# One matmul instead of two for the phases of an S4D kernel: the two constants that round a phase move into the same 32 rows as its parts

## The chip, the cores and the metric

The kernel runs on one core of one Trainium2 chip. The metric is the device time of one execution in microseconds (us), the median of a few runs; lower is better.

## The reference

The layer normalises its input and adds three things: the input itself, an S4D convolution and a gated linear unit. L is 2048 positions, D is 448 channels, N is 256 complex modes for each channel, and F is 1792 hidden features.

```python
xn = layernorm(A_u)                                   # [1, 2048, 448]
# S4D
dt = exp(log_dt);  A = -exp(log_A_real) + 1j * A_imag;  C = (C_real + 1j * C_imag) * dt[:, None]
P = exp((A * dt[:, None])[:, :, None] * arange(2048))
K = 2 * einsum("dn,dnl->dl", C, P).real               # one filter per channel
y = irfft(rfft(xn.T, 4096) * rfft(K, 4096))[:2048].T + xn * D_skip
# GLU
h = sigmoid(xn @ w_gate) * (xn @ w_up)                # [2048, 1792]
out = A_u + y + h @ w_down
```

## The kernel before

Two generators are interleaved by a table of weights. One, `conv`, does the S4D part; the other, `glu`, does the gated unit. A scheduler then fixes the order of the instructions of every engine when the program is built, from its own model of durations. Each engine runs its instructions strictly in that order.

**The GLU.** Every weight and activation is split into a high and a low fp32r part, so that each product takes three matmuls. The matmuls that write `gu` (line 696, 512 columns) are the gate and up products, and the ones that write `po` (line 809, 448 columns) are the products with `w_down`. The GLU runs over the positions in two halves; the crossing from one half to the other, in which the second half of the input is loaded, normalised (`xt`), transposed (line 212) and put through the first stage of a Fourier transform (line 281), falls in the middle of the S4D filter's stage.

**The filter K (`kgen`).** The 448 channels are taken in 56 chunks of 8 channels. For a chunk, PE first makes the phase of every mode at 32 coarse and 32 fine steps, reduced to less than one turn. The matmuls that do this write the tile `tr` (line 526). Their stationary operand is `ph`, which holds the phases of the chunk's channels in high and low parts, and their moving operand is the constant table `sel`. Rounding to whole turns is done inside the matmul's own sum: the large constant `MAGIC` = 1.5 x 2^23 is added to the phase and taken away again, which leaves the nearest whole number. For each of the two halves of the modes (`h`) there are two matmuls of 512 columns which accumulate in one bank of `tr`. The first one (`sel[:, 0]`) gives the whole turns, with the two constants in rows far from the phase's rows. The second one (`sel[:, 1]`) subtracts the phase. That is four matmuls a chunk.

ScalarE then takes absolute value and sines of `tr` (lines 535 to 538, into the tile `S`, of which there are two). VectorE multiplies `S` with the magnitudes `me` and `mf`, which GpSimd makes (line 503), into `Et` (lines 589 and 590, two buffers) and `Ft` (line 591, one buffer). PE contracts `Et` and `Ft` over the modes in 32 pairs of small matmuls (64 rows of the trace) into `ko` (line 603). After every fourth chunk a first Fourier stage follows (line 553). There is one `tr` tile, so the phases of the next chunk can only be written when ScalarE has read those of the chunk before. In the order of PE the phases of chunk c+2 mostly stand right behind the `ko` matmuls of chunk c, and around such a group stand GLU matmuls.

**The phases' way to `ph`.** A preparation stage writes the parts of the phases of all channels to DRAM (`ph_d`, six rows for each channel). `phase_load` (line 475) brings 16 channels, two chunks, into one of the two buffers of `ph`. It is issued on the SyncE queue (SP), right after the phases of a chunk with odd number are made. The same queue carries the loads and stores of the GLU's weights. The rows of `ph` that no load writes hold 1.0, so that `MAGIC` needs only a row in `sel`.

**After `kgen`,** `spectra` multiplies the spectra of filter and input and transforms back; the rest of the GLU runs between its matmuls. SBUF of `sel` is used again for another table there.

Of the kernel before, what the change touches and what calls it, by code (L numbers as in the profile page):

```python
# [11 lines left out]
F32 = mybir.dt.float32  # L12
F32R = mybir.dt.float32r
# [14 lines left out]
MAGIC = 1.5 * 2.0**23  # L28
# [19 lines left out]
DC = 8  # L48
# [7 lines left out]
def _tables():  # L56

    a = np.arange(NA)[:, None]
    k1 = np.arange(NK1)[None, :]
    ang = 2 * np.pi * ((a * k1) % 64) / 64.0  # L60


    wk = np.zeros((4, NA, 2, 2, 32))

    wx = np.zeros((4, NA, 64))
    for j in range(4):
        wk[j, :, 0, j % 2] = np.cos(ang)[:, :32]
        wk[j, :, 1, j % 2] = -np.sin(ang)[:, :32]
        wk[j, :, 1, j % 2, 0] = np.cos(ang)[:, 32]
        wx[j, :, :NK1] = np.cos(ang)  # L70
        wx[j, :, NK1:] = -np.sin(ang)[:, 1:32]
    b = np.arange(NB)[:, None]
    k2 = np.arange(64)[None, :]
    tab = np.zeros((NK1, 128, 128))
    bk = np.zeros((2, 2, 64, 2, 128))
    for q in range(NK1):
        al = 2 * np.pi * ((b * (q + 64 * k2)) % 4096) / 4096.0
        c, s = np.cos(al), np.sin(al)
        tab[q] = np.block([[c, -s], [s, c]])
# [12 lines left out]
    tab = tab[:32].reshape(8, 4, 128, 128).transpose(0, 2, 1, 3)  # L92

    wf = np.zeros((2, 2, 4, 8, 32, NA))
    for k in range(32):
        ang = 2 * np.pi * ((k * (64 * np.arange(NA)[None] + np.arange(64)[:, None])) % 4096) / 4096.0
        re = (1.0 if k == 0 else 2.0) / 4096.0 * np.cos(ang)
        im = -2.0 / 4096.0 * np.sin(ang)
        if k == 0:
            im = np.broadcast_to(np.cos(np.pi * np.arange(NA))[None] / 4096.0, im.shape)  # L100
        wf[:, 0, k % 4, k // 4] = re.reshape(2, 32, NA)
        wf[:, 1, k % 4, k // 4] = im.reshape(2, 32, NA)

    sel = np.zeros((128, 2, 2, DC, 32))
    st = np.arange(32) + 0.5
    for e in range(DC):
        for i in range(2):  # L110
            sel[DC * i + e, 0, 0, e] = st
            sel[64 + DC * i + e, 0, 1, e] = st
            sel[64 + DC * (2 + i) + e, 0, 1, e] = 1.0
    sel[:, 1] = -sel[:, 0]
    for row, tb_, sg in ((16, 1, -1.0), (32, 0, 1.0), (96, 1, 1.0), (97, 0, -1.0)):
        sel[row, 0, tb_] = sg * MAGIC
    f = lambda v, s: np.ascontiguousarray(v.reshape(s).astype(np.float32))
    return {
        "c_wk": f(wk, (128, 2, 64)),
        "c_wx": f(wx, (128, 64)),  # L120
        "c_tab": f(tab, (8, 128, 4, 128)),
        "c_t32": f(t32, (128, 3, 128)),
        "c_bk": f(bk[0], (128, 2, 128)),
        "c_wf": f(wf, (128, 32, NA)),
        "c_sel": f(sel, (128, 2, 512)),
        "c_id": np.eye(128, dtype=np.float32),
    }

# [2 lines left out]
def s4d_glu_kernel(ctx, tc, io):  # L131
    nc = tc.nc
# [8 lines left out]
    ph_d = dram.tile([D, 6, N], F32, name="ph_d")  # L141
# [9 lines left out]
    const = ctx.enter_context(tc.tile_pool(name="const", bufs=1, side="left"))  # L151
# [4 lines left out]
    nc.gpsimd.memset(hpi, math.pi / 2)  # L156
    one = const.tile([128, 1], F32, name="one")
    nc.gpsimd.memset(one, 1.0)
    sel = const.tile([128, 2, 512], F32R, name="sel")
    qpi = const.tile([128, 1], F32, name="qpi")  # L160
    nc.gpsimd.memset(qpi, math.pi / 4)

# [3 lines left out]
    zs = const.tile([128, 16], F32, name="zs")  # L166
# [278 lines left out]
    def kgen(pk):  # L445
# [23 lines left out]

        def phase_load(b):  # L470
            t = pht[b % 2]
            src = ph_d[16 * b : 16 * b + 16].rearrange("(k r) c n -> c r k n", k=2)
            for i in range(6):
                r0 = DC * i if i < 2 else 64 + DC * (i - 2)
                nc.sync.dma_start(t[r0 : r0 + DC].bitcast(F32), src[i])

        mes = [tl["me0"], tl["me1"]]
        nc.gpsimd.memset(mes[0][:, :, 0:1], 1.0)
# [39 lines left out]
        def ahead(cn):  # L518
# [3 lines left out]
            ps = psc[-1].tile([128, 2, 512], F32, name="tr", bufs=1)  # L522
            ph = pht[cn // 2 % 2]
            for h in range(2):
                for i in range(2):
                    nc.tensor.matmul(  # L526
                        ps[:, h], ph[:, cn % 2, 128 * h : 128 * h + 128], sel[:, i],
                        start=(i == 0), stop=(i == 1),
                    )
            if cn % 2 == 1 and cn + 3 < NCK:  # L530
                phase_load(cn // 2 + 2)
            rows = lambda t: t.rearrange("p c (h e) s -> p h c (e s)", h=2)
# [40 lines left out]
        for g in range(NCK // NCH):  # L573
            for c in range(NCH):
                cn = g * NCH + c
# [22 lines left out]
                for q in range(2):  # L598
                    sl = 2 * (cn % 4) + q
                    for k in range(4):  # L600
                        h, cc = k // 2, k % 2
                        for j in range(4):
# [4 lines left out]
                                start=(k == 0),  # L607
                                stop=(k == 3),
# [400 lines left out]
    def conv():  # L1009
        with tc.tile_pool(name="psk", bufs=1, space=PSUM) as ps_, tc.tile_pool(  # L1010
# [9 lines left out]
            with tc.tile_pool(name="pst", bufs=1, side="right", reuse_waits="tile") as pst:  # L1020
# [30 lines left out]
                    xns.append(xn)  # L1051
                    yield Y0[q]

                nc.gpsimd.tensor_copy(sel[:, 0, 0:1], zs[:, 7:8])
# [91 lines left out]
```

## Time and profile before

| | |
|---|---|
| median of 3 runs | 744.78 us (742.77 to 745.26) |
| span of the profiled execution | 746.7 us; nothing is recorded outside of it |
| PE busy | 702.8 us, 94% of the span |
| VectorE, ScalarE, GpSimd busy | 557.8, 423.3 and 348.7 us |
| mean granted TensorE clock | 0.980 |
| phase matmuls (line 526) | 224, from 124.5 us to 543.9 us |
| loads of `ph` (line 475) | 168, 16 KB each |

PE and PEld are the matmuls and the weight loads of TensorE, DVE is VectorE, ACT is ScalarE, POOL is GpSimd and SP is SyncE. A matmul's row goes from its start to the modelled arrival of its result, and the rows of matmuls in a stream overlap. The distance from one matmul's start to the next one's start is what a matmul costs in a stream. In the chain of waits the profile goes back from the last instruction to what released it, and so on; its shares say what the time was spent on. A name followed by q, as SPq, is the engine's queue, which issues DMAs and handles semaphores.

### The profile page before, as it was taken

The numbers are of one execution on the slowest core, as the hardware profiler recorded it, in microseconds if no ns is written. First come the engines' busy times: TensorE is split into PE (matmuls) and PEld (weight loads), VectorE is DVE, ScalarE is ACT, GpSimd is POOL, SyncE is SP. The second block draws the span as 40 slices with busy tenths as digits, with TensorE's granted clock in tenths as the row PEclk, the third lists the DMA queues.
The fourth block names the chain that finished last, engine by engine and source line by source line (L and its number), as shares of the span: only waits on it lengthen the run. The fifth ranks groups of instructions, "written<-read, shape, count | busy, mean of one in ns | idle before, by whom it ended". The sixth has DMA issues, their size and how long they took to land.

```text
span 746.7 us, 19397 instructions
## 1 busy us (share of the span) xinstructions
PE 702.8 (94%) x7892; PEld 553.9 (74%) x7892; DVE 557.8 (75%) x776; ACT 423.3 (57%) x650; POOL 348.7 (47%) x423
## 2 busy tenths in 40 slices
PE   3899998999999899899999999999999999998995
PEld 2666787887877778666788887888877777775784
DVE  5899995789788889868578888877965555565543
ACT  3546383587587768796676786687742222313320
POOL 2110064985765956946545686385844002251002
PEclk9998999999999999999999999999999999999998
DMA  9956347245134444556831331231169999999846
GB/s 209 232 142 170 104 141 230 96 128 173 40 112 142 136 108 120 139 154 189 267 110 63 109 97 64 92 99 67 55 151 259 276 250 228 231 261 228 204 106 166
DMA packets 98952, 114.75 MB, mean 154 GB/s; under 512 B 11888, under 2 KB 86832, under 8 KB 98864
## 3 DMA queue, kind: packets, MB, share of 16 engines
q1 hardware_dynamic: 74704, 89.11, 44.2%
q10 hardware_dynamic: 21584, 18.24, 9.2%
q0 software_dynamic: 2576, 6.17, 3.2%
q8 instruction: 62, 1.02, 0.6%
q14 instruction: 26, 0.21, 0.1%
HBM read 69.64 MB, written 43.84 MB: 152 GB/s over the span
## 4 chain that ended last, share of the span: by engine, by line
PE 68%; DVE 14%; issue 5%; ACT 4%; DMA 4%; POOL 3%; SPq 2%; ACTq 0%; DVEq 0%; POOLq 0%
PE gu L696 28%; PE po L809 13%; PE sp L891 7%; PE tr L526 6%; PE ko L603 6%; PE pv L918 4%; DVE Ft L591 2%; DVE pm L440 1%; PE kp L553 1%; DVE Et L590 1%; DMA sx<-x_d 1%; ACT S L538 1%; DVE hf L707 1%; DVE pl L311 1%; DVE wl L750 1%
## 5 line engine op out<-in xcount | busy, mean ns | idle before, releaser
L503 POOL TENSOR_TENSOR me<-me,pm 128x32 f32<-128x32 f32 (+1 forms) x168 | 135.9, 809 | 134.5 <-DVE Et L590 122.8
L503 POOL TENSOR_TENSOR mf<-mf,pm 128x64 f32<-128x64 f32 (+1 forms) x112 | 107.8, 963 | 4.4
L696 PE MATMUL gu<-xh,wh 128*128 128x512 f32 x336 | 100.0, 406 | 1.5 <-ACT xh L221 0.9
L696 PE MATMUL gu<-xh,wl 128*128 128x512 f32 x336 | 96.9, 396 | 0.0
L696 PE MATMUL gu<-xl,wh 128*128 128x512 f32 x336 | 96.7, 393 | 0.0
L589 DVE TENSOR_TENSOR Et<-me,S 128x1024 f32<-128x1024 f32 x56 | 79.6, 1421 | 17.2 <-ACT S L538 14.4
L590 DVE TENSOR_TENSOR Et<-me,S 128x1024 f32<-128x1024 f32 x56 | 75.9, 1356 | 16.0 <-ACT me L516 9.6
L809 PE MATMUL po<-dh,hh 128*128 128x448 f32 x224 | 85.5, 382 | 1.3 <-DVE hf L707 0.7
L809 PE MATMUL po<-dl,hh 128*128 128x448 f32 x224 | 83.5, 373 | 0.0
L809 PE MATMUL po<-dh,hl 128*128 128x448 f32 x224 | 82.3, 369 | 0.0
L591 DVE TENSOR_TENSOR Ft<-mf,S 128x1024 f32<-128x1024 f32 x56 | 77.6, 1386 | 5.5 <-ACT S L538 4.5
L696 PEld LDWEIGHTS gu<-xh,wh 128*128 128x128 f32 x336 | 62.0, 192 | 21.3 <-issue 4.7
L535 ACT ACTIVATE S<-tr 128x1024 f32<-128x1024 f32 x56 | 57.5, 1027 | 34.6 <-PE tr L526 33.9
L696 PEld LDWEIGHTS gu<-xh,wl 128*128 128x128 f32 x336 | 63.9, 190 | 14.6 <-DVE ys L257 0.7
L603 PEld LDWEIGHTS ko<-Et,Ft 128*32 128x32 f32 x3584 | 53.7, 110 | 28.2 <-issue 12.1
L707 DVE SCALAR_TENSOR_TENSOR hf<-th,gu 128x512 f32<-128x512 f32 x56 | 38.2, 682 | 48.5 <-PE gu L696 38.2
L696 PEld LDWEIGHTS gu<-xl,wh 128*128 128x128 f32 x336 | 63.4, 190 | 14.2 <-issue 0.7
L603 PE MATMUL ko<-Et,Ft 128*32 128x64 f32 x3584 | 64.0, 221 | 9.5 <-DVE Ft L591 7.4
L704 ACT ACTIVATE th<-gu 128x512 f32<-128x512 f32 x56 | 33.7, 601 | 64.8 <-PE gu L696 50.7
L526 PE MATMUL tr<-sel,ph 128*128 128x512 f32 x224 | 66.8, 421 | 2.5 <-DMA ph<-ph_d 2.1
L712 ACT CAST hh<-hf 128x512 fp32r<-128x512 f32 x56 | 34.9, 623 | 56.5 <-DVE hf L707 54.2
L814 DVE SCALAR_TENSOR_TENSOR acc<-po,acc 128x448 f32<-128x448 f32 x80 | 48.2, 617 | 23.1 <-PE po L809 23.1
(198 smaller groups left out, 1340.9 us busy)
## 6 DMA issues: line engine op xcount, KB each, us to landing
sk_d<-sk ACTq DMA_DIRECT2D x14, 512.0 KB
sx<-x_d SPq DMA_DIRECT2D x32, 224.0 KB
skl<-sk_d SPq DMA_DIRECT2D x16, 448.0 KB
vp<-v_d SPq DMA_DIRECT2D x16, 448.0 KB
v_d<-vt SPq DMA_DIRECT2D x62, 112.0 KB
wt_d<-wh SPq DMA_DIRECT2D x9, 512.0 KB
wt_d<-wl SPq DMA_DIRECT2D x9, 512.0 KB
wl<-wt_d SPq DMA_DIRECT2D x9, 512.0 KB
```

Of the source, the lines that this page charges most:

```text
L503: ins = nc.gpsimd.tensor_tensor(m[:, :, w + a : 2 * w : n], m[:, :, a:w:n], par(base + i).unsqueeze(2).to_broadcast([128, 4 * DC, w // n]) ...
L526: nc.tensor.matmul(ps[:, h], ph[:, cn % 2, 128 * h : 128 * h + 128], sel[:, i], start=(i == 0), stop=(i == 1),)
L535: nc.scalar.activation(rows(cs), pv, AF.Abs)
L589: v.tensor_tensor(Et[:, :, :, 32:64], two(me[:, :, 32:64]), S[:, 1::-1], ALU.mult)
L590: v.tensor_tensor(Et[:, :, :, 0:32], two(me[:, :, 0:32]), S[:, 1:3, :, ::-1], ALU.mult)
L591: fts[:] = [v.tensor_tensor(Ft, two(mf), S[:, 3:5], ALU.mult)]
L603: mm = nc.tensor.matmul(ko[32 * j : 32 * j + 32, sl], Ft[:, cc, DC * h + 4 * q + j], Et[:, cc, DC * h + 4 * q + j], start=(k == 0), stop=( ...
L696: glu_mm[:] = [nc.tensor.matmul(ps, a_, b_, start=(n == 0), stop=(n == len(mm) - 1))]
L707: marks[1] = v.scalar_tensor_tensor(hf, th, 1.0, pgu[1], ALU.add, ALU.mult)
L809: glu_mm[:] = [nc.tensor.matmul(po, a_[:, bs], w_, start=(n == 0), stop=(n == 3 * fc - 1))]
L814: v.scalar_tensor_tensor(acc[:, b], po, 0.5, acc[:, b], ALU.mult, ALU.add)
L891: mm = nc.tensor.matmul(to, tb[:kk, t, 64 * c : 64 * c + 64], rhs, start=True, stop=True, skip_group_check=True,)
```

## The change

The table `sel` is laid out anew, with half its size. Of the 128 rows each group of 32 serves two of the chunk's eight channels. In a group stand, in this order: the parts of the two channels (rows 0 to 11, six rows each), a row with +MAGIC, a row with -MAGIC, and the same parts once more with negative sign (rows 14 to 25). One matmul then adds the phase, the constant, takes the constant away, and subtracts the phase. The second matmul of each half of the modes falls away, so a chunk has two phase matmuls and not four; in the whole kernel there are 112 and not 224.

`ph` must hold the parts twice and in groups. `phase_load` issues eight DMAs of 12 partitions and not six of 8 partitions, and each DMA moves 24 KB (12 partitions, two chunks, 1 KB) and not 16 KB. For 16 channels that is 192 KB and not 96 KB.

```diff
-    sel = np.zeros((128, 2, 2, DC, 32))
+    sel = np.zeros((4, 32, 2, DC, 32))
     st = np.arange(32) + 0.5
     for e in range(DC):
-        for i in range(2):
-            sel[DC * i + e, 0, 0, e] = st
-            sel[64 + DC * i + e, 0, 1, e] = st
-            sel[64 + DC * (2 + i) + e, 0, 1, e] = 1.0
-    sel[:, 1] = -sel[:, 0]
-    for row, tb_, sg in ((16, 1, -1.0), (32, 0, 1.0), (96, 1, 1.0), (97, 0, -1.0)):
-        sel[row, 0, tb_] = sg * MAGIC
+        g, r = e // 2, 6 * (e % 2)
+        for at, sg in ((r, 1.0), (r + 14, -1.0)):
+            sel[g, at : at + 2, 0, e] = sg * st
+            sel[g, at + 2 : at + 4, 1, e] = sg * st
+            sel[g, at + 4 : at + 6, 1, e] = sg
+        sel[g, 12, :, e] = MAGIC
+        sel[g, 13, :, e] = -MAGIC
...
-    sel = const.tile([128, 2, 512], F32R, name="sel")
+    sel = const.tile([128, 512], F32R, name="sel")
...
         def phase_load(b):
             t = pht[b % 2]
-            src = ph_d[16 * b : 16 * b + 16].rearrange("(k r) c n -> c r k n", k=2)
-            for i in range(6):
-                r0 = DC * i if i < 2 else 64 + DC * (i - 2)
-                nc.sync.dma_start(t[r0 : r0 + DC].bitcast(F32), src[i])
+            src = ph_d[16 * b : 16 * b + 16].rearrange("(k g e) i n -> g (e i) k n", k=2, g=4)
+            for at in (0, 14):
+                for g in range(4):
+                    r0 = 32 * g + at
+                    nc.sync.dma_start(t[r0 : r0 + 12].bitcast(F32), src[g])
...
             for h in range(2):
-                for i in range(2):
-                    nc.tensor.matmul(
-                        ps[:, h], ph[:, cn % 2, 128 * h : 128 * h + 128], sel[:, i],
-                        start=(i == 0), stop=(i == 1),
-                    )
+                nc.tensor.matmul(ps[:, h], ph[:, cn % 2, 128 * h : 128 * h + 128], sel, start=True, stop=True)
```

Lines behind the edit stand up to three lines higher in the changed kernel: 603 becomes 600, 696 becomes 693, 809 becomes 806. The scheduler makes a new order. Three places of it follow.

PE in the second half of the filter's stage. `xl`, `xr`, `xh` are parts of the normalised input and `wh`, `wl` those of the gate and up weights. Before:

```order
L696 MATMUL gu<-xh,wh 128x512 x3
L696 MATMUL gu<-xr,wh 128x512
L603 MATMUL ko<-Et_1088,Ft 32x64 x32
L526 MATMUL tr<-sel,ph_1096 128x512 x4
L696 MATMUL gu<-xh,wl 128x512 x3
L696 MATMUL gu<-xr,wl 128x512
```

The same place now:

```order
L693 MATMUL gu<-xh,wh 128x512 x3
L693 MATMUL gu<-xr,wh 128x512
L600 MATMUL ko<-Et_1088,Ft 32x64 x32
L526 MATMUL tr<-sel,ph_1096 128x512 x2
L693 MATMUL gu<-xh,wl 128x512 x3
L693 MATMUL gu<-xr,wl 128x512
```

Only the number of phase matmuls differs here; the GLU matmuls around it are the same ones.

PE at the crossing of the GLU's halves. The rows of line 281 and 212 belong to the second half of the input. Before:

```order
L281 MATMUL gu<-xt,wx 64x448 x4
L526 MATMUL tr<-sel,ph_1095 128x512 x4
L281 MATMUL gu<-xt,wx 64x448 x4
L696 MATMUL gu<-xh,wh 128x512 x3
L696 MATMUL gu<-xr,wh 128x512
L696 MATMUL gu<-xh,wl 128x512 x3
L696 MATMUL gu<-xr,wl 128x512
```

At the corresponding place now:

```order
L600 MATMUL ko<-Et_1089,Ft 32x64 x4
L526 MATMUL tr<-sel,ph_1095 128x512 x2
L281 MATMUL gu<-xt,wx 64x448 x4
L212 MATMUL gu<-ident,xt 64x128 x2
L281 MATMUL gu<-xt,wx 64x448 x2
L526 MATMUL tr<-sel,ph_1095 128x512 x2
L600 MATMUL ko<-Et_1088,Ft 32x64 x32
```

The phases of two chunks that share a buffer of `ph` now stand close together, with only eight rows of small matmuls between them.

SP, the queue of the loads, at the first loads of `ph`. `wt_d` is where split weights are kept for the second half. Before:

```order
L631 DMA wraw<-in_B_w_up_dram 64x128 x2
L637 DMA rd<-in_B_w_down_dram 128x448
L475 DMA ph_1095<-ph_d 8x2x256 x6
L475 DMA ph_1096<-ph_d 8x2x256 x6
L753 DMA wt_d<-wh 128x1024
```

and now:

```order
L628 DMA wraw<-in_B_w_up_dram 64x128 x2
L634 DMA rd<-in_B_w_down_dram 128x448
L476 DMA ph_1095<-ph_d 12x2x256 x8
L476 DMA ph_1096<-ph_d 12x2x256 x8
L750 DMA wt_d<-wh 128x1024
```

Two more issues and twice the bytes stand for every two chunks.

More of the change, by code (lines that the diff above doesn't have):

```diff
@@ L124, in _tables @@
         "c_wf": f(wf, (128, 32, NA)),
-        "c_sel": f(sel, (128, 2, 512)),
+        "c_sel": f(sel, (128, 512)),
         "c_id": np.eye(128, dtype=np.float32),
@@ L1052, in conv @@
                     yield Y0[q]
-                nc.gpsimd.tensor_copy(sel[:, 0, 0:1], zs[:, 7:8])
+                nc.gpsimd.tensor_copy(sel[:, 0:1], zs[:, 7:8])
                 nc.gpsimd.dma_start(sel, io["c_sel"])
```

## The prediction

> **What bounds the kernel now.** I read the busy times of the page first, then three stages of the table by windows, then the chain of waits in two of them, and last the timeline around a few groups of phase matmuls.
>
> ```profile
> span 746.7 us, 19397 instructions
> PE 702.8 (94%) x7892; PEld 553.9 (74%) x7892; DVE 557.8 (75%) x776; ACT 423.3 (57%) x650; POOL 348.7 (47%) x423
> ```
>
> PE is busy for 94% of the span. A busy share says nothing of a stage, so the next rows cut the span where the phase matmuls begin, in the middle of the filter's stage, and at its end. The columns are the window, its length, and the busy time of PE, PEld, DVE, ACT and POOL with counts, then the granted clock, the share of the DMA engines and GB/s.
>
> ```profile
> 124.50:350.00 225.50, 214.50 (x2866) 168.78 (x2867) 188.85 (x207) 166.26 (x248) 155.31 (x180) 0.98 0.43 128
> 350.00:555.20 205.20, 205.08 (x3066) 168.43 (x3065) 162.87 (x172) 144.34 (x206) 126.24 (x156) 1.00 0.38 112
> 555.20:747.00 191.80, 178.82 (x1490) 136.20 (x1478) 100.45 (x189) 47.72 (x91) 39.35 (x49) 0.98 0.88 216
> ```
>
> I call them the early half, the late half and the tail. In the late half PE never rests (205.08 of 205.20 us), while DVE works 79% of the time and ACT 70%. In the early half PE rests for 11 us, and DVE is at 84%. The tail has no phase matmul. The chain of waits followed back within the early and the late half, by line:
>
> ```profile
> by line: PE gu L696 16.6%; PE po L809 11.9%; issue 10.4%; PE tr L526 7.0%; PE ko L603 6.7%; DVE Ft L591 5.4%; DVE pm L440 4.2%; DVE Et L590 3.8%; ACT S L538 3.4%; DVE Et L589 2.5%; PE gu L281 2.0%; ACT S L535 2.0%; DVE hf L707 1.7%; DMA xt<
> by line: PE gu L696 44.8%; PE po L809 20.6%; PE tr L526 14.2%; PE ko L603 14.0%; PE kp L553 3.0%; PE kq L553 2.0%; PE ko L613 1.1%; DVE hf L707 0.3%; issue 0.1%; DVEq L707 0.0%
> ```
>
> The late half's chain is PE and nothing else, and the phase matmuls (`tr`, line 526) are 14.2% of it. The early half's chain changes between PE, DVE and ACT, and `tr` has 7.0% of it. So a PE matmul that is left out is worth all of its time in the late half, and part of it in the early half.
>
> **The two matmuls that go.** What one costs in a stream is not its recorded length but the distance to the next start.
>
> ```profile
> 372.23 1.09 PE L526 MATMUL tr<-sel,ph 128*128 128x512 f32 x4
> 373.16 0.85 PE L696 MATMUL gu<-xh,wh 128*128 128x512 f32 x3
> 429.67 1.10 PE L603 MATMUL ko<-Et,Ft 128*32 128x64 f32 x64
> 430.70 1.20 PE L526 MATMUL tr<-sel,ph 128*128 128x512 f32 x4
> 431.73 0.62 PE L696 MATMUL gu<-xh,wl 128*128 128x512 f32 x2
> ```
>
> At 372.23 four phase matmuls take 0.93 us until the next matmul starts, 0.2325 us each. At 430.70, behind the small `ko` matmuls, the four take 1.03 us; the extra 0.10 us belongs to the change of shape, which stays. So I price a removed matmul at 0.2325 us. The Trainium skill (TensorE: Matmul & The Clock Gate, section Back-to-back issue gap) gives 512 columns / 2.4 + 2.5 ns, 216 ns, for a single stream at full clock, and 131 ns sustained for 512 columns with weight loads. By 216 ns the 112 matmuls would be worth 24.2 us and by 131 ns 14.7 us. The row decides: no stream here comes below 0.2325 us for these matmuls.
>
> ```profile
> 124.50:350.00 225.50, 35.69 (x116) 20.85 (x116) 0.98 0.43 128
> 350.00:555.20 205.20, 31.16 (x108) 18.77 (x108) 1.00 0.38 112
> ```
>
> These are the same windows for line 526 alone (PE, then PEld). Late half: 108 matmuls, 54 go, 54 x 0.2325 = 12.6 us, all on the path. Early half: 116 matmuls, 58 go, at most 58 x 0.2325 = 13.5 us. From below, `tr` has 7.0% of 225.5 us on that chain, 15.8 us; half is 7.9 us, and if DVE or ACT holds the rest of the chain back it could come to nothing. I take 7.9 us.
>
> Is there room for the others in the late half, so that they don't become the bound? Per chunk (27 chunks in 205.2 us, 7.6 us each) the change brings 7.1 us.
>
> ```profile
> L589 DVE TENSOR_TENSOR Et<-me,S 128x1024 f32<-128x1024 f32 x56 | 79.6, 1421 | 17.2 <-ACT S L538 14.4
> L590 DVE TENSOR_TENSOR Et<-me,S 128x1024 f32<-128x1024 f32 x56 | 75.9, 1356 | 16.0 <-ACT me L516 9.6
> L591 DVE TENSOR_TENSOR Ft<-mf,S 128x1024 f32<-128x1024 f32 x56 | 77.6, 1386 | 5.5 <-ACT S L538 4.5
> L538 ACT ACTIVATE S<-S,hpi 128x1024 f32<-128x1024 f32 x56 | 65.3, 1167 | 0.0
> L535 ACT ACTIVATE S<-tr 128x1024 f32<-128x1024 f32 x56 | 57.5, 1027 | 34.6 <-PE tr L526 33.9
> L536 ACT ACTIVATE S<-tr 128x1024 f32<-128x1024 f32 x56 | 57.2, 1022 | 0.0
> L537 ACT ACTIVATE S<-tr 128x512 f32<-128x512 f32 x56 | 33.9, 606 | 0.0
> ```
>
> One chunk passes PE (1.0 us), four activations (1.03 + 1.02 + 0.61 + 1.17 = 3.8 us), three products (1.42 + 1.36 + 1.39 = 4.2 us) and 64 rows of `ko` (1.1 us): 10.1 us. The order leaves two chunk periods for it, 15.2 us now and 14.2 us then. DVE's load rises to 162.9 / 192.6 = 85%. Both fit. ACT waits 33.9 us for `tr`, so it gets its work sooner. In the early half DVE would be at 188.9 / 217.6 = 87% with my 7.9 us; that is why I don't take the full 13.5 us.
>
> **The loads of `ph`.** In the order each pair of chunks gets eight issues and not six.
>
> ```profile
> L475 SPq DMA_DIRECT2D ph<-ph_d x168: 263/297/1598, 121.0 to 518.7; - x168
> 431.93 2.08 SPq L475 DMA_DIRECT2D ph<-ph_d  x6
> L526 PEldq EVENT_SEMAPHORE  x136: 51/51/51, 123.7 to 541.9; - x136
>   DMA ph<-ph_d: 2.1, 1
> ```
>
> Six issues at 431.93 take 2.08 us; eight take 2.8 us at the same rate. The work that hides them is two chunks: the load is issued behind one chunk's phases and its data is wanted two chunks' time later, some 14 us. What stands behind them on SP are loads and stores of GLU weights; in the late half PE waits for none of them, and 0.7 us in 14 us of queue doesn't change that. Without the cover it would be 28 x 0.7 = 20 us. Bytes grow by 28 x 96 KB = 2.7 MB, while the DMA engines are at 38 to 43% in these stages. I take 0. Only the first load was waited for (the last row, 2.1 us once); its two more issues cost 0.6 us, against which the order puts five more `po` matmuls ahead of the first phases; 0 again.
>
> The matmul that reads a new `ph` waits for each of its DMAs, and a wait beyond what an instruction holds is a semaphore instruction of 51 ns in PE's own queue. Behind it stand all matmuls of the GLU. Two more of them for 28 loads are at most 28 x 2 x 0.051 = 2.9 us, and 0 if the queue runs ahead. The phases now nearly always stand right behind `ko`, where the queue has just waited for DVE and has little lead, so I take 2.0 us.
>
> **The order at the crossing.** Two groups of phases stand there with 8 + 2 small rows between them.
>
> ```profile
> 303.46 0.99 PE L281 MATMUL gu<-xt,wx 32*64 32x448 f32 x12
> 305.99 1.10 PE L603 MATMUL ko<-Et,Ft 128*32 128x64 f32 x64 [1.53 <-DVE Et L589]
> ```
>
> Twelve small rows take 0.99 us, so ten give about 1.0 us of work, while ACT needs 1.03 + 1.02 + 0.61 = 2.7 us to read the one `tr` tile. PE stands still for 1.7 us there. It had a stop of 1.53 us nearby before, so this may cost nothing (if it replaces it), and it may cost more, since a stop has a second price:
>
> ```profile
> 187.85 1.43 PE L603 MATMUL ko<-Et,Ft 128*32 128x64 f32 x64 [2.27 <-DVE Ft L591]
> 248.97 0.43 PE L603 MATMUL ko<-Et,Ft 128*32 128x64 f32 x16 [2.54 <-DVE Ft L591]
> 185.20:188.40 3.20, 0.93 (x42) 1.00 0.19 45
> 188.50:191.80 3.30, 3.30 (x39) 0.50 0.57 159
> 246.30:249.80 3.50, 0.96 (x66) 1.00 0.08 29
> 250.00:253.20 3.20, 3.20 (x50) 0.50 0.02 5
> ```
>
> After the stops of 2.27 and 2.54 us PE ran at a granted clock of 0.50 for over 3 us, so each lost about 1.6 us more, some 4 us together. The Trainium skill (TensorE: Matmul & The Clock Gate, section HAM oscillation) says that the clock falls after more than about 3.4 us without work. Here it falls after less; the row decides. I take 1.7 us for the crossing, between 0 and 4 us.
>
> The tail's PE order is unchanged and it starts earlier as a whole: 0, with DMA engines at 88%, where a transfer that isn't started earlier could keep 1 us.
>
> **The sum.** 12.6 + 7.9 - 2.0 - 1.7 = 16.8 us off the span of 746.7 us, 729.9 us. The median of the runs, 744.78 us, lies 1.9 us (0.3%) below the span, so the forecast is 744.8 - 16.8 = 728 us. A difference of 0.3%, 2.2 us, is about what a measurement of this kernel can tell from no change.
>
> **Rivals.** First, DVE and ACT keep the early half as long as it is. For it: DVE at 84%, and these rows of the early half's waits (total us, times, longest).
>
> ```profile
> PE ko L603 <- DVE Ft L591: 7.4, 6, 2.5
> DVE Et L589 <- ACT S L538: 8.7, 8, 3.3
> ```
>
> Against it: the wait ACT <- PE `tr` is there too, 33.9 us in all, and phases that start earlier shorten that chain. With nothing from the early half, 12.6 - 2.0 - 1.7 = 8.9 us; with both costs at their worst 5.7 us: about 737 us. Second, all of it counts, because the chain through ACT and DVE begins with the phases and gets shorter by the same 0.465 us for each chunk: 12.6 + 13.5 = 26.1 us and no cost, 719 us. A half-clock stretch that disappears adds 1.6 us.
>
> Third, on the other side: PE comes to wait for ACT and DVE at new places around the crossing and in the early half, since the scheduler moved `ko` and phases among the GLU matmuls, and each such stop of 2.3 to 2.5 us brings its half clock: 4 us each. Beyond the one counted it would take five more (20 us against 16.8) to end slower, 748 us, and eight would give 760 us. For it: the early half has two such stops already, and a closer pace makes more. Against it: PE rests only 11 us in the whole early half, and a stop lets DVE catch up for the next chunks.
>
> Fourth, the change doesn't do what it says in time: the slots that come free fill with waits, because PE's queue, not the array, sets the pace around `ko` (the 0.10 us of shape change and the 2.9 us of semaphores say that it plays a part). Then it stays at 744.8 us. The gap-free row at 372.23 speaks against it.
>
> **Chances.** The forecast's case 0.52, early half lost 0.22, all counts 0.12, slower by stops 0.09, nothing 0.05. The range reaches from the full gain with two half-clock stretches saved, 716 us, to the first rival with its costs at their worst, 740 us with a little of the tail's; it leaves out the last two cases and the edges. Faster by over 0.3% is 0.52 + 0.22 + 0.12 = 0.86, the rest 0.05 and 0.09.
>
> **What would show it.** Right: 112 phase matmuls with 0.23 us between starts; in the late half a window of the same GLU work that is 12 us shorter, with PE still without rest; line 526 at some 7 to 8% of its chain; ACT waiting less for `tr`. Wrong: PE resting for DVE `Ft` in the late half; more than three stretches at 0.50 clock in the filter's stage; a wait of PE or ACT on `ph<-ph_d` after the first one; a tail that is longer than 192 us.

## The result, and the profile after

The changed kernel takes 737.09 us in the median of four runs (735.94 to 740.26), the kernel before 745.02 us beside it: a ratio of 0.9891, with an interval of 0.9852 to 0.9931. Measured once more in the last experiment, it took 740.22 us against 745.75 us, 0.9902 (0.9866 to 0.9937). So it is faster by 5.5 to 8 us, a third to not quite half of the 16.8 us that were forecast.

The head of the page, of the kernel after:

```profile
span 734.2 us, 19242 instructions
PE 682.4 (93%) x7780; PEld 532.7 (73%) x7780; DVE 557.0 (76%) x776; ACT 421.1 (57%) x650; POOL 355.9 (48%) x423
PEclk9999999999999999699999999999999999999998
```

PE has 112 matmuls fewer and is busy for 20.4 us less. The row of the granted clock has a 6 in one slice, at 294 to 312 us, and that will matter.

Equal times of the two kernels don't hold equal work, so I cut both spans at equal work. The GLU has 1904 matmuls, the ones that write `gu` at line 696 (693 after) and `po` at line 809 (806 after), in the same order in both kernels but for three of them. The table has the time at which the n-th one starts:

| start of GLU matmul | chunks whose phases are done | before | after |
|---|---|---|---|
| 400 | 1 | 131.4 | 133.4 |
| 800 | 19 | 271.7 | 267.5 |
| 1000 | 31 | 369.4 | 368.2 |
| 1600 | 56, filter ended | 584.8 | 576.1 |
| end of the span | | 746.7 | 734.2 |

Stage 1 (400 to 800) holds 18 chunks, stage 2 (800 to 1000) is the crossing with 12 chunks, and stage 3 (1000 to 1600) holds the last 25. The same stages in the table by windows (window, length, busy time of PE, PEld, DVE, ACT, POOL with counts, granted clock, DMA share, GB/s), before:

```profile
131.40:271.70 140.30, 134.09 (x1762) 110.10 (x1761) 120.48 (x122) 97.33 (x139) 103.01 (x112) 0.98 0.38 117
271.70:369.40 97.70, 92.92 (x1311) 67.87 (x1310) 77.37 (x93) 76.57 (x122) 59.12 (x77) 0.98 0.58 164
369.40:584.80 215.40, 214.61 (x3059) 174.73 (x3058) 164.65 (x182) 142.41 (x206) 127.30 (x152) 1.00 0.39 116
```

And after:

```profile
133.40:267.50 134.10, 125.86 (x1725) 101.96 (x1724) 118.40 (x119) 95.55 (x136) 99.92 (x104) 0.99 0.40 129
267.50:368.20 100.70, 94.39 (x1288) 65.44 (x1287) 78.58 (x95) 76.02 (x121) 61.78 (x79) 0.93 0.56 163
368.20:576.10 207.90, 203.28 (x3009) 165.53 (x3008) 165.63 (x182) 141.18 (x206) 133.84 (x155) 1.00 0.43 128
```

Stage 1 is 6.2 us shorter, with 37 matmuls fewer. Stage 3 is 7.5 us shorter, with 50 fewer. Stage 2, with 23 fewer, is 3.0 us longer: PE's busy time there goes up and the clock down to 0.93. The start is 2.0 us later, which is chance: this profile has 3.4 us at half clock there (125.3 to 128.7 us), and a second profile of the same kernel (the last experiment), which has none, comes to matmul 400 at 131.6 us. The tail behind matmul 1600 is 3.8 us shorter (161.9 against 158.1 us). 2.0 - 6.2 + 3.0 - 7.5 - 3.8 is the 12.5 us between the two spans. The tail's part is chance as well. In the profile of before, the PE row of the timeline shows

```profile
676.44 1.69 PE L891 MATMUL sp<-skl,tb 128*64 128x224 f32 x8 [2.66 <-ACT vt L924]
```

a stop of 2.66 us, behind which the same eight matmuls take 1.69 us where they took 0.98. The profile of after has no such stop in its tail, but the second profile of it has a tail of 163.4 us. Without that part 8.7 us are left, near the 7.9 us of the medians.

**Stage 3.** PE's busy time falls by 11.3 us (214.61 to 203.28): 50 x 0.2325 is 11.6. But PE, which rested 0.8 us there, now rests 4.6 us. The chain of waits within stage 3, by line, before and after:

```profile
by line: PE gu L696 44.3%; PE po L809 18.1%; PE tr L526 12.6%; PE ko L603 12.4%; PE sp L891 4.4%; PE kp L553 2.9%; PE kq L553 1.9%; PE pv L918 1.6%; PE ko L613 0.9%; DVE hf L707 0.3%; ACT hh L712 0.3%; ACT ks L616 0.3%; issue 0.1%; DVEq L70
by line: PE gu L693 38.9%; PE po L806 16.8%; PE ko L600 11.6%; PE tr L526 6.5%; PE sp L888 4.6%; DVE Ft L588 2.7%; DVE Et L586 2.6%; PE kp L550 2.4%; issue 1.9%; PE pv L915 1.6%; PE kq L550 1.5%; DMA dl<-dt_d 1.1%; DVE Et L587 1.1%; ACT S L
```

`tr` falls from 12.6 to 6.5%, and VectorE's `Ft` and `Et` stand in a chain that was PE alone. PE's waits of this window (total us, times, longest):

```profile
PE ko L600 <- DVE Ft L588: 2.7, 4, 1.6
```

The timeline of PE shows where, and what else came:

```profile
418.38 1.10 PE L600 MATMUL ko<-Et,Ft 128*32 128x64 f32 x64
419.61 0.71 PE L526 MATMUL tr<-sel,ph 128*128 128x512 f32 x2
425.50 1.10 PE L600 MATMUL ko<-Et,Ft 128*32 128x64 f32 x64
426.53 0.73 PE L526 MATMUL tr<-sel,ph 128*128 128x512 f32 x2
427.10 0.84 PE L693 MATMUL gu<-xh,wl 128*128 128x512 f32 x3
...
511.11 0.22 PE L550 MATMUL kq<-wk,ks 64*64 64x64 f32 x1
512.97 1.10 PE L600 MATMUL ko<-Et,Ft 128*32 128x64 f32 x64 [1.64 <-DVE Ft L588]
```

The stops stand behind the small matmuls of the first Fourier stage (line 550), which come every fourth chunk; the longest is the last row. At 426.53 the two phase matmuls take 0.57 us to the next start, 0.465 and the same 0.10 for the change of shape as before. At 419.61 they read a freshly loaded `ph` and start 1.23 us after `ko`, not 1.03: that is the wait for its eight DMAs. Added up in the trace over stage 3, the starts between phase matmuls fall from 19.06 to 7.83 us, the steps from line 550 to `ko` rise from 1.04 to 4.05 us, the steps from `ko` and from line 550 to `tr` rise from 3.21 to 4.65 us, and all the rest gives 0.7 us: -11.2 + 3.0 + 1.4 - 0.7 = -7.5.

**Stage 2, the crossing.** Its chain by line, before and after:

```profile
by line: PE gu L696 26.1%; PE po L809 10.2%; PE ko L603 9.5%; PE tr L526 7.8%; issue 5.9%; DVE Ft L591 5.6%; PE gu L281 4.7%; ACT S L538 3.3%; PE gu L212 2.9%; PE kp L553 2.7%; ACT S L536 2.6%; DVE Et L589 2.6%; DVE Et L590 2.5%; ACT S L535
by line: PE gu L693 11.3%; issue 11.1%; ACT S L535 7.8%; DVE pm L440 7.4%; ACT S L532 5.6%; ACT S L533 5.6%; DVE Ft L588 4.7%; DVE Et L587 4.6%; DVE Et L586 3.9%; DMA xt<-in_A_u_dram 3.3%; ACTq L677 3.0%; ACT S L534 3.0%; ACT x L675 3.0%; D
```

Before, the PE lines shown make 64% of it; after, ScalarE and VectorE hold it and no PE line but `gu` stands near the top. The timeline around the slice with the low clock, and the clock there:

```profile
294.07 0.88 PE L600 MATMUL ko<-Et,Ft 128*32 128x64 f32 x48 [0.94 <-DVE Ft L588]
295.93 0.62 PE L212 MATMUL gu<-ident,xt 128*64 128x128 f32 x2 [0.98 <-DVE xl L222]
```

```profile
292.50:296.10 3.60, 1.67 (x52) 0.98 0.40 139
296.10:309.60 13.50, 13.10 (x113) 0.50 0.28 67
309.80:313.00 3.20, 3.20 (x109) 1.00 0.94 317
```

Two stops of 0.94 and 0.98 us, one for VectorE's `Ft` and one for `xl`, and then PE works for 13.5 us at half its clock. Before, the clock's record has one stretch of 3.4 us at 0.50 in this stage (307.9 to 311.3 us), and now one of 13.7 us. The 10.2 us more at half clock cost up to 5.1 us, nearly what the 23 saved matmuls (5.3 us) are worth. PE's stops grow as well, from 4.8 to 6.3 us (97.70 less 92.92, and 100.70 less 94.39).

**The other signs.** The instructions of line 526 in PE's queue (min, median, max in ns, first and last start), and two rows of the waits, after:

```profile
L526 PEldq EVENT_SEMAPHORE  x160: 51/51/51, 125.7 to 536.8; - x160
```

```profile
ACT S L532 <- PE tr L526: 31.5, 16, 3.4
PE tr L526 <- DMA ph<-ph_d: 0.2, 1, 0.2
```

There are 24 semaphore instructions more ahead of the phases (136 before), ScalarE waits 31.5 us for `tr` (33.9 before), and PE hardly waits for a load of `ph`.

### The profile page after: what moved, and what is told of

Same layout as the page of the kernel before. It is cut to its first block, busy times and chain, and to the rows that moved or that the text cites. A ratio compares the mean times of both kernels' runs of the same rounds, so it can differ in the third digit from the quotient of the medians.

```text
span 734.2 us, 19242 instructions
## 1 busy us (share of the span) xinstructions
PE 682.4 (93%) x7780; PEld 532.7 (73%) x7780; DVE 557.0 (76%) x776; ACT 421.1 (57%) x650; POOL 355.9 (48%) x423
## 4 chain that ended last, share of the span: by engine, by line
PE 55%; DVE 17%; ACT 8%; DMA 8%; issue 5%; POOL 4%; SPq 2%; ACTq 1%; DVEq 0%; POOLq 0%
PE gu L693 23%; PE po L806 13%; PE sp L888 5%; PE ko L600 5%; PE pv L915 3%; PE tr L526 3%; DVE Ft L588 2%; DVE Et L587 2%; ACT S L535 2%; DVE Et L586 2%; DVE pm L440 2%; ACT S L532 1%; DMA sx<-x_d 1%; ACT S L533 1%; DMA tb<-in_c_tab_dram 1%
## 5 line engine op out<-in xcount | busy, mean ns | idle before, releaser
L504 POOL TENSOR_TENSOR me<-me,pm 128x32 f32<-128x32 f32 (+1 forms) x168 | 137.5, 819 | 114.8 <-DVE Et L587 102.9
L504 POOL TENSOR_TENSOR mf<-mf,pm 128x64 f32<-128x64 f32 (+1 forms) x112 | 113.8, 1016 | 5.2
L693 PE MATMUL gu<-xl,wh 128*128 128x512 f32 x336 | 96.2, 394 | 0.0
L586 DVE TENSOR_TENSOR Et<-me,S 128x1024 f32<-128x1024 f32 x56 | 80.1, 1430 | 18.1 <-ACT S L535 17.0
L587 DVE TENSOR_TENSOR Et<-me,S 128x1024 f32<-128x1024 f32 x56 | 78.9, 1410 | 15.4 <-ACT me L517 12.0
L588 DVE TENSOR_TENSOR Ft<-mf,S 128x1024 f32<-128x1024 f32 x56 | 79.3, 1416 | 5.5 <-ACT S L535 4.5
L532 ACT ACTIVATE S<-tr 128x1024 f32<-128x1024 f32 x56 | 57.7, 1030 | 33.2 <-PE tr L526 31.5
L535 ACT ACTIVATE S<-S,hpi 128x1024 f32<-128x1024 f32 x56 | 65.6, 1172 | 0.0
```

Of the source, the lines that this page charges most:

```text
L504: ins = nc.gpsimd.tensor_tensor(m[:, :, w + a : 2 * w : n], m[:, :, a:w:n], par(base + i).unsqueeze(2).to_broadcast([128, 4 * DC, w // n]) ...
L532: nc.scalar.activation(rows(cs), pv, AF.Abs)
L535: sins[:] = [nc.scalar.activation(cs, cs, AF.Sin, scale=-TWO_PI, bias=hpi)]
L586: v.tensor_tensor(Et[:, :, :, 32:64], two(me[:, :, 32:64]), S[:, 1::-1], ALU.mult)
L587: v.tensor_tensor(Et[:, :, :, 0:32], two(me[:, :, 0:32]), S[:, 1:3, :, ::-1], ALU.mult)
L588: fts[:] = [v.tensor_tensor(Ft, two(mf), S[:, 3:5], ALU.mult)]
```

## The experiments

Each ratio is to the kernel before, run beside it. The marks are the starts of GLU matmuls 800, 1000 and 1600, as above. PE's work up to each is the same, except for the phase matmuls that an edit takes out or puts in, the two other paces, and one chunk's `ko` in the second experiment. Code shown is cut: `ph[...]` stands for the operand as before, `mf16` and `me16` for the first 16 columns, broadcast as in the line replaced.

**The loads without the shorter sum.** The changed kernel with a second table of zeros, so that each half of the modes takes two matmuls again:

```diff
-                nc.tensor.matmul(ps[:, h], ph[...], sel, start=True, stop=True)
+                for i in range(2):
+                    nc.tensor.matmul(ps[:, h], ph[...], sel[:, i], start=(i == 0), stop=(i == 1))
```

> The changed kernel with its new table and its eight loads, and with the second matmul of each half put back, against a table of zeros (so 224 phase matmuls). It differs from the kernel before in the loads of ph alone. Theory A (the removed matmuls gave PE about 25 us, and most of what is missing came back as waits of PE for VectorE and as half clock): the loads cost at most the 2 to 3 us of semaphores, 745 to 748 us. Rival B (the missing 9 us against the forecast are the price of the eight loads, in PE's queue and on SP): about 754 us.

747.12 us, 1.0000 (0.9971 to 1.0029). Stage 3 of it:

```profile
368.70:585.80 217.10, 214.78 (x3060) 174.69 (x3059) 165.82 (x182) 142.09 (x205) 128.32 (x154) 1.00 0.41 121
```

Eight loads and the new rows of `ph` cost nothing that the median shows; in stage 3 PE rests 2.3 us and not 0.8, most of it in the steps from `ko` and from the first Fourier stage to `tr`, which grow from 3.21 to 4.43 us. Its crossing, with four matmuls, is no longer than before and has no half clock:

```profile
272.20:368.70 96.50, 91.51 (x1311) 66.70 (x1311) 78.07 (x93) 75.22 (x120) 58.16 (x75) 1.00 0.60 172
```

**The shorter sum without the loads.** The kernel before with its first matmul alone (`sel[:, 0]`):

```diff
-                for i in range(2):
-                    nc.tensor.matmul(ps[:, h], ph[...], sel[:, i], start=(i == 0), stop=(i == 1))
+                nc.tensor.matmul(ps[:, h], ph[...], sel[:, 0], start=True, stop=True)
```

> The kernel before with the second phase matmul of each half left out (the phase is not subtracted), and with its six loads. Theory A: it gains hardly more than the change, 734 to 737 us, with waits of PE for Ft and Et as in the changed kernel. Rival B: the full forecast gain without the loads' price, 728 us or less.

740.05 us, 0.9883 (0.9829 to 0.9936), as the changed kernel. Marks 265.2, 367.6, 577.8: stage 1 gains 6.1 us, stage 2 loses 4.7, stage 3 gains 5.2. About 1 us of the first two is one chunk's `ko`, which this order has behind matmul 800 and the others ahead of it. So what was lost of the gain is not lost to the loads.

**One load.** Sixteen rows for each channel in DRAM, written twice, so that 16 channels come in one DMA:

```diff
-            for at in (0, 14):
-                for g in range(4):
-                    nc.sync.dma_start(t[32 * g + at : 32 * g + at + 12].bitcast(F32), src[g])
+            nc.sync.dma_start(t.bitcast(F32), src)
```

> The changed kernel with the phases stored in DRAM in the order of ph's 128 rows, ones included, so that a pair of chunks is loaded by one DMA of 256 KB and not by eight of 24 KB; the stores to DRAM double in the preparation. The sum within each group of 32 rows has one pair of constants per channel. Theory A: only the waits for eight DMAs in PE's queue go (the stretch from ko to tr was 0.28 us in the mean after and 0.21 before), 2 to 4 us: 733 to 735 us. Rival B: all of the loads' price goes, 728 us.

749.92 us, 1.0029 (1.0000 to 1.0057). The loss lies ahead of the filter: GLU matmul 300 starts at 121.2 us, 14.5 us later than after the change (106.7), and matmul 1600 at 589.6, 13.5 us later. The preparation writes twice as many pieces, and PE has 17 us at half clock by matmul 300 where it had 6.8. From there to matmul 1600 one load is 1 us faster, where theory A put 2 to 4 us.

**Less work for VectorE.** To see whether VectorE holds back the gain, `Ft` is computed for half its columns, in the changed kernel and in the kernel before:

```diff
-                fts[:] = [v.tensor_tensor(Ft, two(mf), S[:, 3:5], ALU.mult)]
+                fts[:] = [v.tensor_tensor(Ft[:, :, :, 0:16], mf16, S[:, 3:5, :, 0:16], ALU.mult)]
```

> The changed kernel with VectorE's product Ft made for half of the fine steps alone (the other half of Ft stays zero), about 0.7 us less of VectorE for each of 56 chunks. Theory A (the freed PE time is eaten where VectorE and ScalarE set the pace): the change is worth more when they have less to do; this kernel runs 15 us or more below its twin with four matmuls, at 720 us or less. Rival C (what is missing is chance of the new order and of the clock, not VectorE's load): still 8 us below its twin, 730 us or more.

> The twin: the kernel before with the product Ft made for half of the fine steps alone. Theory A: it gains little, since its late half waits for PE alone; some 5 us from the early half and the crossing, 738 to 742 us. Rival C: it gains as much as the changed kernel does from the same cut.

726.60 us, 0.9701 (0.9655 to 0.9746), with the change; 749.65 us, 1.0011 (0.9980 to 1.0043), without it. The two are 23 us apart, nearly the second rival's full gain. The stages of the first:

```profile
132.20:261.70 129.50, 124.30 (x1725) 101.96 (x1724) 108.16 (x120) 98.47 (x140) 88.96 (x109) 0.99 0.43 135
261.70:357.90 96.20, 89.73 (x1287) 64.60 (x1286) 70.77 (x93) 72.69 (x118) 51.52 (x77) 0.96 0.60 170
357.90:565.70 207.80, 203.24 (x3010) 165.33 (x3008) 153.51 (x182) 142.43 (x207) 112.85 (x154) 1.00 0.44 129
```

Stage 1 gives 4.6 us more and stage 2 4.5 us more than after the change alone; stage 3 is as it was (207.8 and 207.9), though VectorE has 12 us less to do there: PE still waits for `Ft` behind the first Fourier stage, 0.64 us at 420.1 and 1.10 us at 475.8 us. So those stops are not VectorE's load alone.

**The same with another piece of VectorE's work.** The second product of `Et` for 16 of its 32 columns:

```diff
-                v.tensor_tensor(Et[:, :, :, 0:32], two(me[:, :, 0:32]), S[:, 1:3, :, ::-1], ALU.mult)
+                v.tensor_tensor(Et[:, :, :, 0:16], me16, S[:, 1:3, :, 31:15:-1], ALU.mult)
```

> The changed kernel with another cut of VectorE's load, as large as the first: the second product into Et is made for half of the fine steps alone (that half of Et's first 32 columns stays zero). Theory A (VectorE takes the gain back): as with the halved Ft, about 727 us and some 20 us below its twin. Rival C (the halved Ft met a lucky order): near the changed kernel, 735 to 740 us, 8 us or so below its twin.

> The twin: the kernel before with the same cut. Both theories: within 3 us of the kernel before, since PE sets its pace in the late half and the halved Ft did nothing for it.

731.76 us, 0.9830 (0.9791 to 0.9869), with the change; 740.89 us, 0.9949 (0.9923 to 0.9974), without it. Now the kernel before gains too, and the two are only 9 us apart. The crossing of both, the changed one first:

```profile
265.70:362.00 96.30, 93.42 (x1287) 65.84 (x1287) 69.00 (x89) 73.20 (x119) 51.54 (x70) 0.96 0.61 172
```

```profile
271.30:364.50 93.20, 90.78 (x1311) 66.21 (x1310) 69.59 (x90) 71.21 (x115) 57.26 (x74) 1.00 0.58 165
```

With four matmuls a chunk this crossing takes 93.2 us, with two 96.3 us. So the first pair's 23 us do not show that VectorE alone eats the gain; that reading fell with the second pair.

**Where the matmuls are saved.** The second matmul (of zeros) only for the 12 chunks of the crossing, or only for the others:

```diff
+                m = 2 if 19 <= cn < 31 else 1        # the other kernel: if not 19 <= cn < 31
+                for i in range(m):
...
```

> The changed kernel with the second matmul (a table of zeros) put back in chunks 19 to 30 alone, those of the crossing of the GLU's halves, where the changed kernel's PE was 3 us later and not 5.5 us earlier. If PE does not set the pace there (theory A), these 24 matmuls cost nothing or give time back, 732 to 737 us. If it does, they cost 24 x 0.23 = 5.6 us, 743 us.

> The complement: two matmuls in chunks 19 to 30, four (one against zeros) in all the others. Theory A: no gain against the kernel before, 744 to 748 us. If PE sets the pace there: 5.6 us below it, 739 to 740 us.

737.95 us, 0.9852 (0.9800 to 0.9904), with four at the crossing; 748.98 us, 1.0011 (0.9975 to 1.0046), with two only there. The crossing of each:

```profile
266.00:366.10 100.10, 93.03 (x1311) 67.61 (x1310) 78.71 (x95) 77.03 (x122) 62.77 (x82) 0.98 0.59 168
```

```profile
272.80:372.50 99.70, 93.94 (x1287) 68.11 (x1286) 78.15 (x92) 72.45 (x117) 53.56 (x71) 0.91 0.57 163
```

This is the clearest pair. The matmuls saved at the crossing bring no time, and those saved elsewhere bring all of the change's gain. It doesn't show that PE has no part in the crossing's length, since two different things make up the loss. The first kernel has the same matmuls and the same 3.4 us at half clock there as the kernel before, but comes to it 5.7 us sooner and stays 2.4 us longer: PE rests 7.1 us and not 4.8. The second comes no sooner than the kernel with new loads and four matmuls (272.8 and 272.2 us) and has hardly more stops (5.8 and 5.0 us), but 17.1 us at half clock where that one has none. This costs up to 8.5 us, more than the 5.3 us saved.

**Work moved from VectorE to GpSimd.** The powers of line 440 as two GpSimd instructions, and the low part `hl` of line 711 on GpSimd, each in the changed kernel:

```diff
-            v.scalar_tensor_tensor(pm[:, j], w, 2.0, w, ALU.add, ALU.mult)
+            nc.gpsimd.tensor_scalar(pm[:, j], w, 2.0, None, ALU.add)
+            nc.gpsimd.tensor_tensor(pm[:, j], pm[:, j], w, ALU.mult)
```

```diff
-            v.tensor_tensor(hl, hf, hh, ALU.subtract)
+            nc.gpsimd.tensor_tensor(hl, hf, hh, ALU.subtract)
```

> The changed kernel with the 70 power steps of pm (0.54 us each on VectorE, 37 us in all) made by GpSimd, two instructions each. Theory A (VectorE's load in the filter's stage takes back what PE was given): about the relief of the halved Ft, so 10 us below the changed kernel, 727 to 730 us, if GpSimd (48% busy) keeps up. Rival: GpSimd's strict order makes the magnitudes late, and PE waits for Et and Ft through it, 740 us or more.

> The changed kernel with the low part of the GLU's product (hl, 56 instructions of 0.87 us on VectorE) made by GpSimd. Theory A: VectorE is relieved by about 30 us within the filter's stage, 728 to 732 us. Rival: the low part comes later and stands between GpSimd's magnitudes, so the matmuls that need it wait, 740 us or more.

783.42 us, 1.0510 (1.0486 to 1.0534), and 765.31 us, 1.0269 (1.0233 to 1.0305). For `hl`, the operation on VectorE after the change and on GpSimd here (min, median, max in ns), and who waits for it:

```profile
L711 DVE TENSOR_TENSOR hl<-hf,hh x56: 634/693/2644, 27.1 to 701.3; 128x512 fp32r<-128x512 f32 x56
```

```profile
L711 POOL TENSOR_TENSOR hl<-hf,hh x56: 1258/1337/5931, 27.0 to 728.7; 128x512 fp32r<-128x512 f32 x56
DVE hf L704 <- POOL hl L711: 32.7, 11, 4.7
```

The operation takes nearly twice as long (once 5.9 us), and VectorE, which was to be relieved, waits 32.7 us for it. Neither run says whether VectorE bounds the crossing; they only say that moving these two pieces to GpSimd costs more than it brings.

**Another pace.** The weight of the filter against the GLU in the interleaving table, 6.0 and 5.0 in place of 5.5, in the changed kernel:

```diff
-WK = 5.5
+WK = 6.0        # the other kernel: 5.0
```

> The changed kernel with the weight of a chunk against the GLU raised from 5.5 to 6.0, so that more GLU matmuls stand between two chunks and VectorE and ScalarE get more time for each, while less of the GLU is left for the tail. Theory A: fewer stops before ko, but some 20 to 30 matmuls fewer to fill the tail, 733 to 740 us. Rival (the order, not the pace, made the stops): anything, with as many stops as before.

> The changed kernel with the weight of a chunk lowered from 5.5 to 5.0, so that fewer GLU matmuls stand between two chunks and more of the GLU is left for the tail. Theory A: more stops before ko, 740 to 750 us. Rival (PE still sets the pace): the same as the changed kernel, 737 us.

747.30 us, 1.0007 (0.9965 to 1.0049), and 737.12 us, 0.9889 (0.9860 to 0.9919). The weight in use is as good as the smaller one, and the larger one loses the whole gain. The crossing ends at 369.0 and 366.4 us, so what the two differ in lies behind it. Both times came out on the other side of theory A's ranges. Each weight makes another order as well as another pace, and which of the two costs the 10 us isn't told apart.

**Four loads.** The parts in two DRAM tensors, so that 16 channels' `ph` comes in four DMAs (two of 16 and two of 32 partitions):

```diff
+            for d, r0, n in ((pa_d, 0, 16), (pb_d, 32, 32), (pa_d, 66, 16), (pb_d, 96, 32)):
+                src = d[16 * b : 16 * b + 16].rearrange("(k e) i n -> (e i) k n", k=2)
+                nc.sync.dma_start(t[r0 : r0 + n].bitcast(F32), src)
```

> The changed kernel with four DMAs for each load of ph and not eight: the parts lie in two DRAM tensors and the rows of a part stand together (two DMAs of 16 partitions, two of 32; the same bytes; the constants stand in the third group of 32 rows). If the waits for eight DMAs in PE's own queue take back what the table of starts shows behind ko (8.4 us against 4.8 before), some 3 us come back: 733 to 735 us. Rival: they are hidden, and the time stays with the changed kernel's run of this call.

> The changed kernel itself once more, beside the four loads and with more rounds, for a narrower interval: 737 us.

738.23 us, 0.9884 (0.9847 to 0.9921); beside it the changed kernel, 740.22 us, 0.9902 (0.9866 to 0.9937). The crossing with four loads:

```profile
262.60:368.60 106.00, 90.88 (x1287) 65.52 (x1286) 82.30 (x95) 78.13 (x125) 69.88 (x85) 0.95 0.53 150
```

It comes to the crossing 2.6 us sooner than any other kernel with VectorE's full work at this pace, and leaves it at 368.6 us, as late as all. PE rests 15.1 us in it. The waits that the edit aimed at do go: the steps from `ko` to `tr` take 4.0 us in sum (26 of them), against 9.0 us (30) in the changed kernel beside it. But the 2.0 us between the two medians lie within the intervals, so whether those waits cost time isn't settled. No version that does the whole work beats the changed kernel by more than the intervals.

All marks together, of the kernels with VectorE's full work and the same pace, and then of the four with a cut. The kernel with one load, whose marks are 10 to 14 us later than the changed kernel's, is left out. The last column is the time at a granted clock of 0.50 in stage 2, from the trace's record of the clock:

| kernel | 800 | 1000 | 1600 | stage 2 | stage 3 | stage 2 at 0.50 |
|---|---|---|---|---|---|---|
| before | 271.7 | 369.4 | 584.8 | 97.7 | 215.4 | 3.4 |
| new loads, four matmuls | 272.2 | 368.7 | 585.8 | 96.5 | 217.1 | 0 |
| two only at the crossing | 272.8 | 372.5 | 589.9 | 99.7 | 217.4 | 17.1 |
| after | 267.5 | 368.2 | 576.1 | 100.7 | 207.9 | 13.7 |
| after, second profile | 266.6 | 367.9 | 576.4 | 101.3 | 208.5 | 13.7 |
| two matmuls, old loads | 265.2 | 367.6 | 577.8 | 102.4 | 210.2 | 13.7 |
| four only at the crossing | 266.0 | 366.1 | 574.5 | 100.1 | 208.4 | 3.4 |
| four loads | 262.6 | 368.6 | 575.7 | 106.0 | 207.1 | 10.2 |
| before, less `Ft` | 273.6 | 371.2 | 586.6 | 97.6 | 215.4 | 3.4 |
| before, less `Et` | 271.3 | 364.5 | 581.2 | 93.2 | 216.7 | 0 |
| after, less `Et` | 265.7 | 362.0 | 571.2 | 96.3 | 209.2 | 6.8 |
| after, less `Ft` | 261.7 | 357.9 | 565.7 | 96.2 | 207.8 | 6.8 |

Three things stand out. Stage 3 takes 215 to 217 us with four matmuls and 207 to 210 with two, whatever VectorE has to do. And the first eight kernels come to the crossing within a range of 10 us, but leave it within 6.4 us: on the whole, whoever comes sooner stays longer. And every kernel of the table with four matmuls at the crossing has at most 3.4 us at half clock there, while those with two have 6.8 to 17.1 us. Why the shorter phases bring more half clock isn't shown; the kernel with `hl` on GpSimd, not in the table, has two matmuls and only 3.4 us. Of the four cuts of VectorE's work three move the end of the crossing forward, by 5 to 10 us, and one doesn't.

## Why the prediction was partly right, step by step

**The price of a matmul: right.** In stage 3, where both kernels run at full clock, the starts between phase matmuls fall from 19.06 to 7.83 us: 11.2 us for 50 matmuls, 0.225 each against 0.2325. Single steps go down to 0.226 us, so the sentence that none comes below 0.2325 holds for the group shown and not for every one. The 131 ns of the sustained figure that was cited is not seen here.

**The late half, 12.6 us: mis-sized.** For the 50 matmuls of stage 3 the term gives 11.6 us, less some 0.9 us for their share of the semaphores. Stage 3 gives 7.5 us, and 6.9 us in the second profile. PE's work did fall by 11.3 us. The step that failed is the room for the others: the prediction compared one chunk's mean time through all engines (10.1 us) with two mean periods (14.2 us) and found that both fit. But the order is not even. At some of the chunks where the first Fourier stage stands ahead of `ko`, PE comes to `ko` before VectorE has made `Ft`, and waits: 3.0 us back. The sign named for it, PE resting for `Ft` in the late half, is there, 4 times and 2.7 us.

**The semaphores, 2.0 us: nearly right.** With new loads and four matmuls, all steps into the first phase matmul of a chunk, without the very first, take 2.0 us more in sum than before; the 23 of them that come from `ko` grow from 4.8 to 6.3 us. In the changed kernel the steps from `ko` to `tr` come to 8.4 us, but there are 30. The instructions are 24 more, of 51 ns each (1.2 us), and not the 56 of the prediction's upper bound. In the medians the 2.0 us don't show.

**The early half, 7.9 us, and the crossing, 1.7 us: the steps that failed.** By matmul 1000 the changed kernel is ahead by 1.2 us (1.5 in the second profile), where the two terms promised some 6. The 18 chunks of stage 1 do give 6.2 us of the 8.6 that their 37 matmuls are worth, 72% (5.3 us and 62% in the second profile), where the prediction took 59% of the early half's 13.5. But the crossing, in which 5.3 us should have been gained in full or in part, loses 3.0 (3.6 in the second profile). The prediction treated the crossing as one stop beside one group of phases. That stop is not where the time went:

```profile
345.51 0.74 PE L526 MATMUL tr<-sel,ph 128*128 128x512 f32 x2 [0.36 <-ACT S L534]
```

It costs 0.36 us and not 1.7: the trace has 14 small rows between the two groups and not ten, and they take PE from 342.92 to 345.15 us. But the crossing is a stage of 100 us with 12 chunks, and the sum had no term for half clock and stops in the rest of it. From 124 us to the last `ko`, both profiles of the changed kernel have 20.5 us at 0.50, and the kernel before has 10.2. The difference, up to 5.1 us, is what the crossing alone has more; the stops there are 1.5 us longer. The pair with the matmuls saved only there, or only elsewhere, shows that at the crossing they bring nothing. The start, taken as 0, was right but for chance.

**The loads: right.** New loads with the old sum give 1.0000. The tail: right, 0 but for chance.

**The rivals.** The first, that VectorE and ScalarE keep the early half as long as it is, gave 737 us, and that is what came. Its account is right in the net (1.2 us by matmul 1000) but not in its detail: most of the early half does get shorter, and the crossing takes most of it back. The second, all of it counts, is seen only where VectorE has less `Ft` to do, and not with less `Et`. The third, stops with half clock around the crossing, is what happened there, though the sign named for it, more than three stretches in the filter's stage, did not come: from 124 us on there are three, as before, but the one at the crossing is four times as long. It makes the stage 3.0 us longer, far from the 20 us at which this rival would have decided. The fourth is out, as stage 3 shows.

**What stays open.** What fixes the end of the crossing near 366 to 372 us isn't settled. Its chain alternates between ScalarE's `S`, VectorE's products and powers, and the input's loads; VectorE is at 78% there and ScalarE at 75%, so neither is full. Three cuts of four speak for VectorE as a part of it; that it alone holds the change's gain back isn't shown, because one cut made the two kernels 23 us apart and the other 9. How much of the loss is the clock's, and what makes the clock stay low for longer with two matmuls, is open too: no run kept the clock up with the order unchanged. Each edit also makes another order, and the two paces are 10 us apart.

## What to carry to other kernels

Price a removed matmul by the distance between starts, and then ask stage by stage whether PE sets the pace there: it is worth its full price only where PE never rests, and even there a cover that is wide enough in the mean can be too short at the one chunk in four with an uneven order. Compare two kernels at marks of equal work, not at equal times; where a stage ends at the same time, however early it begins, add up its stops and its time at half clock before naming another engine as the bound. Undo the change in one stage and keep it in the others: that told more here than taking work from another engine, though both make another order.

## What the hardware showed that was not expected

The clock fell to 0.50 after two stops of 0.94 and 0.98 us within 2.8 us and stayed there for 13.7 us; before the change, stops of 2.27 and 2.54 us were each followed by some 3.4 us at 0.50. The Trainium skill (TensorE: Matmul & The Clock Gate, section A second HAM failure mode: psum-queue depth-cycling) tells of a kernel whose frequent short rests between groups made the clock swing; this trace agrees, at 0.98 before and 0.50 after such a pair. The second profile has the same: stops of 1.01 and 0.99 us, and then 13.7 us. But such stops don't always do it: with new loads and four matmuls, stops of 0.89 and 1.55 us (301.4 and 306.1 us) were followed by none. In all 17 profiles the stretches at 0.50 last 3.41, 6.83, 10.24 or 13.65 us, multiples of 3.41; only the last one, which the end of the span cuts off, does not.

A matmul that waits for more DMAs starts later, but only from some number on: the first phase matmul starts 149 ns after the last `ko` matmul where it waits for no load, and also where its 16 channels came in one DMA or in four; with six it mostly starts after 238 ns and with eight after 343 to 345 ns.
